# An attention and GLU block on one core: subtractions and stores of the down weights one key tile later, the guard's transpose one key tile sooner

## The chip, the cores and the metric

The kernel runs on one core of a Trainium2 chip. The metric is the device time of one execution in microseconds (us). A core has five engines: TensorE (PE, matrix products), VectorE (DVE), ScalarE (ACT), GpSimd (POOL) and SyncE (SP). Each runs its instructions in the order in which the program gives them, and they wait for one another through semaphores. SP issues nearly all transfers here; POOL issues some.

## What is computed

One block of a transformer in float32: layer norm, attention with 32 heads that share one key head and one value head, a residual sum, layer norm, a gated product without a nonlinearity, and a second residual sum. S = 2048 tokens, D = 576, head size 18, F = 4608.

```
x = A_x
h = x + attention(layernorm(x), wq, wk, wv, wo)   # softmax of q k / sqrt(18), keys and values shared by the 32 heads
n = layernorm(h)
out = h + ((n @ w_gate) * (n @ w_up)) @ w_down
```

## The kernel before

Queries are taken in four blocks of 512 tokens, heads in eight groups of four, keys in 16 tiles of 128. A **pair** (`pair`, line 674) is two heads of one group on one key tile: two score products of 56 rows each (line 694), then one exponential on ScalarE over 128 x 1024 numbers (line 695). Two pairs finish a key tile of a group, and `flush` (line 702) gives the value products of a finished key tile to PE (line 699), one key tile behind the scores. This stage, attention over the first query block, is where the change lies.

Beside the pairs, in the same stage, the loop in `run` (from line 1600) gives out three kinds of other work, and it is the program's own order on each engine that fixes when each is tried; no scheduler reorders it. One turn of the loop is a **step**: a pair, some query work, a pair, then waiting small jobs (`run_aux`, line 750), `flush`, and one `next(work)`, which is one step of the down weights.

- **Query work** (`queries`, line 473). The queries of all blocks are products of the normed tokens with the query weights, in tiles of 126 rows; each tile takes 14 rounds of two products (line 498, into the banks `psq` and `psr`, for the two halves of the rows). A round counts 1, the end of a tile 4, and a step hands out 2.3 (`RATE`, line 1659). At the end of a tile VectorE empties the banks: line 505 copies `psr`, line 506 adds `psq` to it, lines 507, 508 and 515 make the parts that are stored. The two banks come from one ring of two, so the next tile's first product into `psq` waits for line 505 and its first into `psr` for line 506. SP stores the tile (lines 510 and 511).
- **Bounds** (`bounds`, line 522). From each block's queries an upper bound of the scores is made, and its largest value is collected in `mx`. `flag` (line 562) reduces `mx` on DVE (line 566), transposes the result on PE (line 569, `psx`), and compares it (lines 571 and 573). Every engine reads that flag at the `guard` (lines 575 to 580), which branches around a repair that is not taken here. `flag` is a generator: `next(flag)` gives out the first reduction, `drain(flag)` the transpose and the rest.
- **Down weights** (`down_weights`, line 1491). In 18 blocks `p`, each of 128 x 4 x 288 numbers, the weights of the last product are loaded (`load`, by POOL, line 1515), combined (`sums`, POOL, line 1521), rounded to the format of the products (`high`, POOL's cast, line 1529), the rounding error is taken (`low(p, i)`, a subtraction on DVE, line 1535, in two spans `i`), and both parts go back to memory (`store`, two transfers by SP, line 1541), for the later stages to read. Block `p` is placed by `begin(p)`: step 6p up to block 10, then 5 apart. From there `load` stands 3 steps before (5 after block 10), `sums` at 0 and 1, `high` at 2, `low` at 4 and 5, `store` at 6. The room of a block is one of two up to block 9, of three after that, so the load of block p waits until store(p - 2), later store(p - 3), has landed.

After the loop, `run` gives out `next(flag)`, then two more steps, drains what is left of the down weights (nothing, the loop has 106 steps), gives out `drain(flag)`, goes on to the end of the seventh group, one pair of pairs more, and the guard.

Of the kernel before, what the change touches and what calls it, by code (L numbers as in the profile page):

```python
# [57 lines left out]
class Block:  # L58
# [1432 lines left out]
    def down_weights(self):  # L1491

        pool, dve, sp = self.nc.gpsimd, self.dve, self.sp
        rooms = [(self.hp.tile([P, 8, HD], F32, tag="h", name="wd_src"), self.hp.tile([P, 8, HD], F32R, tag="h", name="wd_hi"))]
        at, where = {}, {}

        def begin(p):  # L1500
            return 6 * min(p, 10) + 5 * max(p - 10, 0)

        def room(p):
            n = p % 2 if p < 10 else (2, 0, 1)[(p - 10) % 3]
            if p in (1, 5, 10):
                home, tag = {1: (self.otp, "oT"), 5: (self.p0q, "XT0"), 10: (self.p0q, "XT1")}[p]
                if p > 1:
                    self.XT[p // 5 - 1] = None
                e = home.tile([P, 9 * TB], F32R, tag=tag, name=f"wd_room{p}").rearrange("p (k j d) -> p k j d", k=2, d=HD)
                rooms[n:] = [(f32(e[:, 0]), e[:, 1])]  # L1510
            return rooms[n]

        def load(p):
            where[p] = room(p)
            pool.dma_start(where[p][0][:, 0:4], self.wd[p])

        def sums(p, i):
            src, _ = where[p]
            if p < NC - 1:
                for i, x, y in ((4, 0, 1), (5, 3, 4), (6, 3, 0), (7, 2, 5))[i:i + 2]:  # L1520
                    pool.tensor_tensor(src[:, i], src[:, x], src[:, y], ALU.subtract)

        def spans(p):
            return [(1, 4), (4, 8)] if p < NC - 1 else [(0, 4)]

        def high(p):
            src, hi = where[p]
            for lo, to in spans(p):
                pool.tensor_copy(hi[:, lo:to], src[:, lo:to])

        def low(p, i):

            src, hi = where[p]
            for lo, to in spans(p)[i:i + 1]:
                dve.tensor_tensor(src[:, lo:to], src[:, lo:to], f32(hi[:, lo:to]), ALU.subtract)

        def store(p):
            src, hi = where.pop(p)
            lo, to = spans(p)[0][0], spans(p)[-1][1]
            for k, t in enumerate((f32(hi), src)):  # L1540
                sp.dma_start(self.wd_dram[p, :, 0:to - lo, k], t[:, lo:to])
            if p in (3, NC - 2):
                del rooms[1:]

        for p in range(NC):
            if p > 10:
                at.setdefault(begin(p) - 5, []).insert(0, lambda p=p: load(p))
            else:
                at.setdefault(max(begin(p) - 3, -1), []).append(lambda p=p: load(p))
            for d, f in ((6, lambda p=p: store(p)), (0, lambda p=p: sums(p, 0)), (1, lambda p=p: sums(p, 2)),  # L1550
                         (2, lambda p=p: high(p)), (4, lambda p=p: low(p, 0)), (5, lambda p=p: low(p, 1))):
                at.setdefault(max(begin(p) + d, -1), []).append(f)
        for k in range(-1, max(at) + 1):
            for f in at.pop(k, ()):
                f()
            yield

    def run(self):
# [17 lines left out]
        with ExitStack() as st:  # L1576
            pool = lambda name, bufs, **k: st.enter_context(tc.tile_pool(name=name, bufs=bufs, **k))
            cp, self.lp, self.hp = pool("const", 1), pool("ln", 2), pool("resid", 2)
            self.qp, self.pp, self.op, self.otp = pool("q", 2), pool("P", P_BUFS), pool("o", 1), pool("oT", 1)
            self.ps = pool("ps", 1, space=PSUM)  # L1580
            self.C = cp.tile([P, C_W], F32, name="C")
            self.ident = self.C[:, C_ID:C_ID + P]
            self.kT = cp.tile([P, S], F32R, name="kT")
            self.V = cp.tile([P, NT, 32], F32, name="V")
            self.mx = cp.tile([H, 8], F32, name="mx")
            st.enter_context(tc.manual_schedule())
            with tc.tile_pool(name="p0q", bufs=1) as self.p0q:
                self.wq_in, self.wq = self.wq, {}
                self.XT = [self.p0q.tile([P, 9, TB], F32R, tag=f"XT{b}", name=f"XT{b}") for b in range(NB)]
                self.G = self.p0q.tile([P, 64], F32R, name="G")  # L1590
                with tc.tile_pool(name="qb", bufs=2) as self.qb:
                    first = self.keys_values()
                    work = self.down_weights()
                    next(work)

                    def rest():
                        yield from first
                        for b in range(1, NB):
                            yield from self.queries(b)
                    self.cast = self.dve.tensor_copy  # L1600
                    others, live, due = rest(), True, 0.0
                    while live:
                        self.pair()
                        due += RATE
                        while due > 0 and live:
                            z = next(others, None)
                            live = z is not None
                            due -= z or 0
                        self.pair()
                        self.run_aux(1)  # L1610
                        self.flush(len(self.pend) - 1)
                        next(work, None)
            assert self.n_mx <= 8
            flag = self.flag()
            next(flag)
            self.wp, self.hh, self.p2 = pool("w", 2), pool("hid", 4), pool("P2", P2_BUFS)
            n = self.n_pair + 4
            self.steps(lambda: self.n_pair < n, work)
            drain(work)
            drain(flag)  # L1620
            self.steps(lambda: self.n_pair % (2 * NT))
            assert self.n_pair == 2 * NT * (NG - 1)
            self.pair()
            self.pair()
            self.flush(len(self.pend) - 1)
            self.guard()
            wo_parts, n = self.load_wo_0(), self.n_pair
            self.load_x(0)
            self.wo_from = n + 12
            self.steps(lambda: self.n_pair < n + 8)  # L1630
            wo_parts()
            del wo_parts
            self.steps(lambda: self.more(0))
            self.load_w(0)
            self.load_wd(WD_BUFS - NQ)
            self.load_x(1)
            self.fill(2.0, 1)
            while 0 not in self.normed:
                self.run_aux(1)
                self.fill(1.0, 1)  # L1640
            while self.n_pair % 8 != 6:
                self.pair()
                if self.n_pair % 8 in (0, 2, 4):
                    self.flush(len(self.pend) - 1)
            self.normal(0)
            self.split_w(0)
            self.load_w(1)
            self.cast = self.act.copy
            drain(self.spread(0))
            self.flush(len(self.pend))  # L1650
            self.pair()
            del self.oT
            self.room()
            self.load_wd(WD_BUFS - 2)
            for b in range(NB - 1):
                self.ffn(b)
# [55 lines left out]
def f32(ap):  # L1712
    return ap.bitcast(F32)
# [20 lines left out]
def drain(gen):  # L1734
    for _ in gen:
        pass
# [85 lines left out]
```

## Time and profile before

| | |
|---|---|
| median of three runs | 2248.4 us (2247.45 to 2248.42) |
| the profiled execution | 2249.98 us, of which the span is 2248.1 us |
| PE busy | 2224.7 us, 99% of the span |
| ACT, DVE, POOL busy | 1436.3 us (64%), 1374.9 us (61%), 899.2 us (40%) |
| mean granted clock of PE | 0.998 |
| the chain that ended last, by engine | PE 85%, DVE 1%, all others about 0% |

The page counts as busy the time in which an engine executes; an instruction that waits for a semaphore is idle time, and the views name who ended it. PE at 99% says that the kernel is bounded by matrix products nearly throughout, so what can be gained is in PE's few gaps and in the stretches in which its clock is granted at less than full speed. Views in order of time merge equal instructions that follow one another into one line with a count.

### The profile page before, as it was taken

How to read it: one execution, taken by the hardware profiler on the slowest of the kernel's cores; microseconds unless marked ns; L12 is line 12 of the kernel's file. 1: busy time of each engine (PE TensorE's matmuls, PEld its weight loads, DVE VectorE, ACT ScalarE, POOL GpSimd, SP SyncE). 2: the span in 40 equal slices, each digit the busy share in tenths (PEclk: the TensorE clock that was granted, in tenths of full speed). 3: DMA queues.
4: the chain of work that ended last, by engine and by line, in shares of the span. 5: the costliest groups of instructions: out<-in, count | busy, mean ns of one | idle time of the engine just before them, and what ended most of it. 6: DMA issues, size and time to landing. Idle time of an engine off the chain costs nothing.

```text
span 2248.1 us, 45954 instructions
## 1 busy us (share of the span) xinstructions
PE 2224.7 (99%) x17958; PEld 1634.8 (73%) x17958; DVE 1374.9 (61%) x2209; ACT 1436.3 (64%) x1950; POOL 899.2 (40%) x976
## 2 busy tenths in 40 slices
PE   7999999999999999999999999999999999999999
PEld 5333335777777777777777777777777888999999
DVE  8555645555655566455555566546455677888776
ACT  7889877666666666666665667565666534555553
POOL 4445401444444444244444435433332455322222
PEclk9999999999999999999999999999999999999999
DMA  5879843545555554655455555564343445677775
GB/s 176 268 230 297 292 169 88 179 153 166 164 173 165 174 181 142 188 167 172 148 177 172 164 162 173 164 207 148 109 121 105 135 161 199 222 236 241 234 248 174
DMA packets 200625, 407.01 MB, mean 181 GB/s; under 512 B 22573, under 2 KB 54445, under 8 KB 200405
## 3 DMA queue, kind: packets, MB, share of 16 engines
q1 hardware_dynamic: 197813, 393.42, 54.6%
q0 software_dynamic: 2592, 10.62, 1.5%
q8 instruction: 143, 2.34, 0.4%
q14 instruction: 77, 0.63, 0.1%
HBM read 317.27 MB, written 74.55 MB: 174 GB/s over the span
## 4 chain that ended last, share of the span: by engine, by line
PE 85%; DVE 1%; ACT 0%; issue 0%; DMA 0%; POOL 0%; SPq 0%; ACTq 0%; DVEq 0%
PE pg L1106 19%; PE acc L699 16%; PE y L1046 13%; PE s L694 9%; PE gs L1332 8%; PE pu L1106 6%; PE yq L1298 4%; PE gu L1106 4%; PE yo L874 3%; PE gs L1339 2%; PE y L1013 1%; PE tx L936 0%; ACT P L695 0%; DVE room L97 0%; PE ye L1458 0%
## 5 line engine op out<-in xcount | busy, mean ns | idle before, releaser
L695 ACT ACTIVATE P<-s 128x1024 f32<-128x1024 f32 x1024 | 1010.1, 1028 | 218.5 <-PE s L694 134.7
L1106 PE MATMUL pg<-X,ws 64*128 64x512 f32 x2511 | 679.6, 389 | 0.5 <-DVE os L725 0.2
L1106 PE MATMUL pu<-X,ws 64*128 64x512 f32 x2511 | 679.8, 389 | 0.0
L1106 PEld LDWEIGHTS pg<-X,ws 64*128 64x128 f32 x2511 | 465.0, 185 | 65.9 <-issue 2.3
L699 PE MATMUL acc<-P,V 128*32 128x512 f32 x4096 | 481.3, 599 | 0.1
L1106 PEld LDWEIGHTS pu<-X,ws 64*128 64x128 f32 x2511 | 464.5, 185 | 16.7
L694 PE MATMUL s<-q,kT 56*128 56x512 f32 x2048 | 425.4, 415 | 5.8 <-ACT P L695 3.6
L1056 POOL TENSOR_TENSOR h<-h,tmp 128x288 f32<-128x288 f32 x320 | 259.1, 841 | 321.8 <-ACT tmp L1055 320.6
L1055 ACT COPY tmp<-y 128x288 f32<-128x288 f32 x320 | 127.9, 400 | 338.5 <-PE y L1046 308.7
L694 PEld LDWEIGHTS s<-q,kT 56*128 56x128 f32 x2048 | 197.8, 184 | 173.8 <-ACT P L695 124.9
L1046 PEld LDWEIGHTS y<-wdo,room 128*128 128x128 f32 x2142 | 289.4, 188 | 40.9 <-issue 38.2
L1046 PE MATMUL y<-wdo,room 128*128 128x288 f32 x2142 | 302.7, 300 | 0.1
L699 PEld LDWEIGHTS acc<-P,V 128*32 128x32 f32 x4096 | 114.4, 109 | 253.9 <-issue 250.8
L1052 DVE TENSOR_TENSOR h<-h,y 128x288 f32<-128x288 f32 x394 | 169.5, 453 | 181.8 <-PE y L1046 178.1
L971 DVE TENSOR_TENSOR ws<-wr,ws 128x1152 fp32r<-128x1152 f32 x108 | 188.7, 1747 | 105.0 <-POOL ws L968 103.6
L1144 DVE TENSOR_TENSOR hf<-pu,hf 128x512 f32<-128x512 f32 x93 | 63.7, 684 | 221.0 <-ACT hf L1140 221.0
L968 POOL CAST ws<-wr 128x1152 fp32r<-128x1152 f32 x108 | 130.8, 1211 | 146.8 <-DMA wr<-in_wgu_dram 119.6
L96 POOL CAST room<-hf 128x256 fp32r<-128x256 f32 (+1 forms) x92 | 58.5, 636 | 314.6 <-DVE hf L1144 314.6
L1281 POOL TENSOR_TENSOR wsum<-wsum,wsum 128x512 f32<-128x512 f32 x72 | 145.2, 2017 | 48.0 <-DMA wsum<-in_wgs_dram 36.0
L97 DVE TENSOR_TENSOR room<-hf,room 128x256 fp32r<-128x256 f32 (+1 forms) x108 | 96.1, 890 | 3.3 <-ACT room L96 1.8
L1106 PE MATMUL gu<-X,ws 64*128 64x512 f32 x810 | 94.5, 389 | 0.0
L1106 PEld LDWEIGHTS gu<-X,ws 64*128 64x128 f32 x810 | 76.5, 184 | 15.7 <-issue 1.3
(267 smaller groups left out, 2762.1 us busy)
## 6 DMA issues: line engine op xcount, KB each, us to landing
wdo<-wd_dram SPq DMA_DIRECT2D x492, 288.0 KB
wr<-in_wgu_dram SPq DMA_DIRECT2D x108, 576.0 KB
wsum<-in_wgs_dram SPq DMA_DIRECT2D x108, 256.0 KB
wd_dram<-wd_room SPq DMA_DIRECT2D x20, 1008.0 KB
wsum_dram<-wsum SPq DMA_DIRECT2D x72, 256.0 KB
raw<-wsum_dram SPq DMA_DIRECT2D x72, 256.0 KB
q<-q_dram SPq DMA_DIRECT2D x64, 216.0 KB
raw<-in_wgs_dram SPq DMA_DIRECT2D x54, 256.0 KB
```

The costliest lines, as they stand in the source:

```text
L694: self.pe.matmul(s_[:, i], self.kT[o:o + 56, t * P:(t + 1) * P], q[o:o + 56, pr], start=True, stop=True)
L695: self.act.activation(p_, s_, AF.Exp, scale=SCALE)
L699: self.pe.matmul(acc[32 * j:32 * j + 32, :], self.V[:, t, :], Ps[j // 2][:, j % 2, :], start=first, stop=last, skip_group_check=True)
L968: self.nc.gpsimd.tensor_copy(w[:, 0], self.wr[n])
L971: self.dve.tensor_tensor(w[:, 1], self.wr.pop(n), f32(w[:, 0]), ALU.subtract)
L1046: pe.matmul(y[:, :HD], m[:, t * P:(t + 1) * P], k, start=(first and j == 0), stop=(j == 2), skip_group_check=True)
L1052: dve.tensor_tensor(hs, hs, y[:, :HD], ALU.add)
L1055: act.copy(z, y[:, :HD])
L1056: pool.tensor_tensor(hs, hs, z, ALU.add)
L1106: pe.matmul(ps, w[o:o + 64, wk, c], X[o:o + 64, xk, c], start=(j == 0), stop=(j == 26))
L1281: pool.tensor_tensor(to, x, y, op)
L1332: pe.matmul(bank[:, g * HT:(g + 1) * HT], W[:, wk, c, g], X[:, 2 * xk + c], start=(first and g == c == wk == xk == 0), stop=(c == 1 and wk ...
```

## The change

Two constants in the placing of `store` and `low` grow by one, and one in the number of pairs before `drain(flag)` shrinks by two. `store(p)` goes from step begin(p) + 6 to + 7, the two subtractions from + 4 and + 5 to + 5 and + 6. Loads, sums and casts stay. `drain(flag)` comes after one step in place of two; the pairs themselves are unchanged in number.

```diff
--- before.py
+++ after.py
@@ -1547,8 +1547,8 @@
                 at.setdefault(begin(p) - 5, []).insert(0, lambda p=p: load(p))
             else:
                 at.setdefault(max(begin(p) - 3, -1), []).append(lambda p=p: load(p))
-            for d, f in ((6, lambda p=p: store(p)), (0, lambda p=p: sums(p, 0)), (1, lambda p=p: sums(p, 2)),
-                         (2, lambda p=p: high(p)), (4, lambda p=p: low(p, 0)), (5, lambda p=p: low(p, 1))):
+            for d, f in ((7, lambda p=p: store(p)), (0, lambda p=p: sums(p, 0)), (1, lambda p=p: sums(p, 2)),
+                         (2, lambda p=p: high(p)), (5, lambda p=p: low(p, 0)), (6, lambda p=p: low(p, 1))):
                 at.setdefault(max(begin(p) + d, -1), []).append(f)
         for k in range(-1, max(at) + 1):
             for f in at.pop(k, ()):
@@ -1614,7 +1614,7 @@
             flag = self.flag()
             next(flag)
             self.wp, self.hh, self.p2 = pool("w", 2), pool("hid", 4), pool("P2", P2_BUFS)
-            n = self.n_pair + 4
+            n = self.n_pair + 2
             self.steps(lambda: self.n_pair < n, work)
             drain(work)
             drain(flag)
```

## Rows read from the trace of the kernel before

**Rows 1.** TensorE's waits from 54 to 300 us: who waited for whom, us, times, longest us.

```profile
PE s L694 <- ACT P L695: 1.8, 7, 0.4
PE s L694 <- DVEq L580: 1.6, 1, 1.6
PE psq L498 <- DVE qs L505: 0.9, 1, 0.9
PE psr L498 <- DVE qs L506: 0.2, 1, 0.2
```

**Rows 2.** Busy us by engine in stretches, then PE clock, DMA share, GB/s.

```profile
136.18:139.60 3.42, 3.42 (x17) 1.29 (x16) 3.42 (x4) 1.41 (x2) 1.77 (x2) 0.50 0.74 251
...
300.02:303.44 3.42, 3.42 (x16) 0.70 (x12) 2.93 (x4) 2.20 (x3) 2.42 (x4) 0.50 1.03 398
```

**Rows 3.** TensorE in order of time around 134 us: start, us, operation [idle before <-releaser].

```profile
131.98 0.40 PE L498 MATMUL psq<-XT,wq 64*126 64x512 f32 x1
...
134.96 0.49 PE L498 MATMUL psq<-XT,wq 64*126 64x512 f32 x1 [0.92 <-DVE qs L505]
135.69 0.50 PE L498 MATMUL psr<-XT,wq 64*126 64x512 f32 x1 [0.23 <-DVE qs L506]
...
140.01 1.07 PE L699 MATMUL acc<-P,V 128*32 128x512 f32 x8
```

**Rows 4.** TensorE in order of time, another tile boundary, from 168 us.

```profile
168.31 0.39 PE L498 MATMUL psq<-XT,wq 64*126 64x512 f32 x1
...
171.00 1.07 PE L699 MATMUL acc<-P,V 128*32 128x512 f32 x8
...
173.12 1.06 PE L699 MATMUL acc<-P,V 128*32 128x512 f32 x8
```

**Rows 5.** VectorE in order of time, 96 to 150 us.

```profile
105.44 2.31 DVE L1535 TENSOR_TENSOR wd_room<-wd_room 128x864 f32<-128x864 f32 x2
115.32 0.69 DVE L505 COPY qs<-psr 126x512 f32<-126x512 f32 x1 [7.57 <-PE psr L498]
...
132.34 1.97 DVE L1535 TENSOR_TENSOR wd_room<-wd_room 128x864 f32<-128x864 f32 x1 [7.66 <-POOL wd_room L1529]
134.23 0.68 DVE L505 COPY qs<-psr 126x512 f32<-126x512 f32 x1
...
137.34 1.35 DVE L1535 TENSOR_TENSOR wd_room<-wd_room 128x1152 f32<-128x1152 f32 x1
```

**Rows 6.** VectorE in order of time, 150 to 200 us.

```profile
165.46 1.32 DVE L1535 TENSOR_TENSOR wd_room<-wd_room 128x1152 f32<-128x1152 f32 x1
168.75 0.69 DVE L505 COPY qs<-psr 126x512 f32<-126x512 f32 x1 [1.97 <-PE psr L498]
```

**Rows 7.** SyncE's queue in order of time, 50 to 110 us.

```profile
74.66 0.57 SPq L1541 DMA_DIRECT2D wd_dram<-wd_src  x1
75.67 3.25 SPq L1541 DMA_DIRECT2D wd_dram<-wd_room  x2
86.95 0.31 SPq L510 DMA_DIRECT2D q_dram<-qs  x1
```

**Rows 8.** GpSimd in order of time, 50 to 110 us.

```profile
82.19 0.57 POOL L1515 DMA_DIRECT2D wd_src<-in_wd_dram  x1 [6.55 <-DMA wd_dram<-wd_src]
...
94.96 0.57 POOL L1515 DMA_DIRECT2D wd_room<-in_wd_dram  x1
```

**Rows 9.** All engines in order of time at the flag and the guard.

```profile
290.54 1.06 PE L699 MATMUL acc<-P,V 128*32 128x512 f32 x8
290.56 0.15 DVE L566 TENSOR_REDUCE mx<-mx 32x1 f32<-32x7 f32 x1
...
293.88 0.18 PE L569 MATMUL psx<-C,mx 32*1 32x32 f32 x1
...
299.64 0.91 PE L694 MATMUL s<-q,kT 56*128 56x512 f32 x4 [1.57 <-DVEq L580]
```

**Rows 10.** The tile `flag`: reads of it, ns min/median/max, first and last start us.

```profile
L579 DVEq TENSOR_LOAD <-flag x1: 542/542/542, 298.1 to 298.1; - x1
```

## The prediction

> **What bounds the kernel now.** I read the page first and then, for the stretch that the diff touches, what ended TensorE's idle time. The change lies inside the first attention, whose loop runs from about 54 us to the guard at about 300 us of a span of 2248.1 us. In these 246 us TensorE (PE) waited for others 1.8 + 1.6 + 0.9 + 0.2 = 4.5 us [rows 1]. So this stretch is PE's own work, and an edit that moves only VectorE (DVE), GpSimd (POOL) and SyncE (SP) work can win no more than these 4.5 us and what follows from them. The reader should see three kinds: 1.8 us in 7 short waits for ScalarE, which are the pace of the softmax; 1.6 us in one wait at the guard; 0.9 + 0.2 us in one place, where PE waits for DVE to empty the two banks of a query tile. In the table by stretch, two stretches of 3.4 us show a granted clock of 0.50, that is 1.2 GHz in place of 2.4: one begins at 136.18 us, the other at 300.02 us [rows 2]. Each comes right behind one of these two waits: the queries' at 134.04 to 135.69 us, the guard's just before 299.64 us [rows 3, 9].
>
> **What the query wait costs now.** The same run of PE work, from the last products of a query tile to the third group of value products behind it, takes 140.01 - 131.98 = 8.03 us here [rows 3] and 173.12 - 168.31 = 4.81 us at another tile boundary [rows 4]. The difference is 3.2 us: 0.92 + 0.23 us of waiting, up to 3.42 / 2 = 1.7 us from the half clock, and the rest because the tile's two halves, issued as a pair, ran one after the other (134.96 and 135.69 us [rows 3]). PE is full on both sides, so I count all 3.2 us as path.
>
> Why DVE was late stands in its order. The last product ended at 131.98 + 0.40 = 132.38 us, but the copy that frees the first bank (line 505) began at 134.23 us, 1.85 us late [rows 3, 5]. Ahead of it stood a subtraction of block 5, low(5, 0). That one had kept DVE idle for 7.66 us, until POOL's cast of the same block came, and then ran 1.97 us [rows 5]. The other subtraction of that block, low(5, 1), came at 137.34 us, behind the tile's operations [rows 5].
>
> **The subtractions a step later.** Block p is due at begin(p) = 6p up to block 10, then 5 apart. low(5, 0) goes from step 34 to 35 and low(5, 1) from 35 to 36. Within a step the loop issues query work before down-weight work; low(5, 1) of step 35 stands behind this tile in the trace, so the tile belongs to step 35, and low(5, 0) now falls behind it too. DVE is then free at 132.4 us, the copy starts on time, and the 3.2 us go. low(5, 0) starts at about 132.4 + (137.34 - 134.23) = 135.5 us, its cast long done, and the pair ends some 2.3 us later (as the pair at 105.44 us [rows 5]), at 137.8 us, no later than before (137.34 + 1.3). Nothing downstream of block 5 is later for that.
>
> The other 34 subtractions: counted through the loop (2.3 units of query work a step, 17 units a tile, 28 of them left when it begins), the tiles' copies stand in steps 5, 13, 20, 27, 35, 42, 50, 57, 64, 72, 79, 86, 94 and 101. Only low(0, 0), low(5, 0), low(6, 1) and low(14, 1) pass behind a tile; none passes ahead of one. What moves closer to a tile is dangerous only if it ends late. Nearest is block 7: low(7, 0) goes from 46 to 47, behind the normalisation of that step, so that both subtractions begin where low(7, 1) began, at 165.46 us [rows 6]. With 2.31 us for a pair that DVE does alone [rows 5] they end at 167.8 us; the copy of that tile is due at 168.75 us [rows 6], so 0.95 us is left. With 1.97 us for the first, as beside a POOL cast [rows 5], they end at about 168.75 us, just in time. I take the first: POOL waits for a transfer there. (The Trainium skill, "SBUF — State Buffer", section "Who interferes with whom", says that a DVE instruction with two inputs in SBUF contends with a GpSimd one that reads SBUF, and that issue order decides who blocks; the 1.97 against about 1.0 us agree. By it the later place, with the casts done, makes the subtractions shorter, and the sum stays as it is.)
>
> **The stores a step later.** A step is about 2.1 us (171.00 to 173.12 [rows 4]). Each of the 36 store transfers goes behind what SP is given in the next step. The largest slip is store(1), from step 12 to 13, where a query tile's store stands first in the queue: from 75.67 us to behind the transfers at 86.95 us, so to about 88 us [rows 7]. POOL's load of block 3 reuses that room and waits for it. store(0)'s second transfer began at 74.66 us and released POOL at 82.19 us, 7.5 us [rows 7, 8]; with that, store(1) is landed at about 96 to 97 us and the load goes out 1 to 2 us later than at 94.96 us [rows 8]. low(3, 0) at 105.44 us was not waiting for POOL [rows 5], and behind that pair DVE is idle for 7.57 us before the next tile at 115.32 us [rows 5], which covers the slip. Later stores wait for DVE or for query stores in the queue now and slip a step or less. Cost: 0 on the path; without that cover each us is paid as under the ring below. Query and mask stores and ob copies, which were behind a store, go a little earlier; no PE wait names them [rows 1].
>
> **The flag's transpose two pairs sooner.** Nothing is added or removed. The products it now follows end at 290.54 + 1.06 = 291.60 us; the maximum it reads is done at 290.56 + 0.15 = 290.71 us [rows 9], so it has 0.9 us to spare; if DVE were later than that, PE with the score products behind it would wait the rest. It frees SP and POOL at the guard some 2 us sooner, and the loads of the output weights with them; no PE wait in [rows 1] is theirs. It doesn't shorten the guard: PE starts again at 299.64 us when DVE has passed its branch [rows 9], and DVE reads the flag only at 298.1 us [rows 10], 4 us after the transpose at 293.88 us [rows 9], because the last accumulator's transpose stands ahead of it. I count 0; between -0.2 and +0.2 us, its own length of 0.18 us [rows 9], as it leaves a full place or lands in one.
>
> **Sum.** -3.2 + 0 + 0 + 0 = -3.2 us. The profiled execution took 2249.98 us for a span of 2248.1 us, so it would be 2246.8; against the median of the three runs, 2248.4 us, I forecast 2245.2 us. My own range for this case is 2244.4 to 2246.2.
>
> **Rivals.**
> The half clock behind the guard goes too: if the stretch at 300.02 us ran at the full clock, up to another 3.42 / 2 = 1.7 us is won, 2243.5 us. Against it: the guard's wait stays as it is.
>
> The half clock behind the queries is not in the median run: then only 3.2 - 1.7 = 1.5 us is won, 2246.7 us. For it: three runs within 1 us can't tell. (The Trainium skill, "TensorE: Matmul & The Clock Gate", section "What's actually happening", says that where the clock changes isn't tied to the kernel's start and varies from run to run; by that rule this rival or the last can hold. The trace shows one execution and neither agrees nor disagrees.)
>
> The stall only moves: block 7's pair ends 1 us late and PE stalls at the tile of 168.75 us instead, or the change reaches nothing on PE: 2248.4 us.
>
> Slower, through the ring of rooms. Up to block 9, block p's load waits for store(p - 2). Two such waits are in [rows 8]: 6.55 us at 82.19, and 94.96 us with none. If every store slips its whole step of 2.1 us and no slack takes it up, block 7, three turns on, is 6.4 us late: 166.8 + 6.4 = 173.2 us for the end of low(7, 1), and the copy due at 168.75 us is 4.4 us late. At 134.23 us a copy 1.85 us late cost 3.2 us, 1.35 us more than its lateness, so this costs 5.8 us and the net is +2.6 us, 2251.0 us. It decides from the point where low(7, 1) ends after 168.75 us. Against it: the slack found at block 3.
>
> **How the numbers follow.** What a measurement of this kernel can tell from no change is about 0.2%, 4.5 us. Forecast 0.60; guard's clock too 0.12; only 1.5 us 0.08; stall moves or nothing 0.12; ring 0.08. Faster by over 0.2% is below 2243.9 us: nearly all of the second case, 0.12. Slower by over 0.2% is above 2252.9 us: a ring that also reaches the tile after next, 0.04. Within: 0.84. The range takes in the forecast's own bounds, the guard's clock and the cases around no change: 2243.2 to 2249.0 us; outside stay the ring and little more.
>
> **What would show it.** Right: no PE wait for the queries' copies at about 134 us, low(5, 0) behind that tile on DVE, the run of PE work 4.8 us long, a granted clock of 1.00 there, the guard's wait near 1.6 us. Wrong: a new PE wait for line 505 or 506 at a tile boundary; DVE waits for POOL's casts of blocks 6 to 9 that grew; a wait of PE for the maximum at the flag's transpose; or all this as said and a time that didn't move.

## The result, and the profile after

| | before | after |
|---|---|---|
| median | 2247.2 us (15 runs, 2244.81 to 2251.52) | 2252.2 us (15 runs, 2250.14 to 2256.23) |
| the profiled execution | 2249.98 us, span 2248.1 | 2256.23 us, span 2253.9 |
| mean granted clock of PE | 0.998 | 0.996 |

The ratio is 1.0024, 95% interval [1.0016, 1.0032]: the change costs 4.9 us where I had forecast a gain of 3.2. Both profiled executions lie above their medians, before by 2.7 us and after by 4.1 us, so a size read from one of them is not yet the size of the median.

TensorE's waits from 54 to 310 us in the profile after (who waited for whom, us, times, longest us), to be held against [rows 1]:

```profile
PE psq L498 <- DVE qs L505: 3.4, 1, 3.4
PE s L694 <- ACT P L695: 3.1, 8, 1.4
PE s L694 <- DVEq L580: 1.6, 1, 1.6
```

Three things are to be seen. The wait for line 506 is gone, and the one for line 505 is 3.4 us long in place of 0.9, at another tile. The waits for ScalarE have grown, and one of them is 1.4 us long where none was above 0.4. The guard's 1.6 us stand. In order of time on TensorE (start, us, operation, idle before and its releaser), the old place and the new one:

```profile
131.88 0.40 PE L498 MATMUL psq<-XT,wq 64*126 64x512 f32 x1
...
136.69 1.07 PE L699 MATMUL acc<-P,V 128*32 128x512 f32 x8
...
146.99 0.39 PE L498 MATMUL psq<-XT,wq 64*126 64x512 f32 x1
...
154.35 0.79 PE L498 MATMUL psq<-XT,wq 64*126 64x512 f32 x1 [3.42 <-DVE qs L505]
...
156.65 1.94 PE L699 MATMUL acc<-P,V 128*32 128x512 f32 x8
...
160.27 1.06 PE L699 MATMUL acc<-P,V 128*32 128x512 f32 x8
```

At the old place the run from the last query products to the third group of value products now takes 136.69 - 131.88 = 4.81 us, to the hundredth what another boundary took [rows 4], and no longer 8.03 [rows 3]. The forecast gain is there. It is given back 14 us later: at the next tile, whose last products start at 146.99 us, PE stops for 3.42 us, and then matrix products take 0.79 and 1.94 us that take 0.39 and 1.06 elsewhere. The table by stretch (start:end, length, busy us of PE, of the weight loads, DVE, ACT, POOL with their counts, granted clock, DMA share, GB/s) says why:

```profile
134.00:140.00 6.00, 6.00 (x46) 2.19 (x46) 4.76 (x7) 5.63 (x7) 0.57 (x1) 1.00 1.03 350
153.09:159.92 6.83, 5.57 (x20) 2.46 (x22) 5.49 (x7) 1.50 (x2) 3.58 (x4) 0.50 0.64 214
303.28:310.10 6.82, 5.67 (x24) 1.43 (x24) 6.09 (x10) 3.75 (x4) 3.76 (x5) 0.50 0.91 333
```

The half clock of 136.18 us [rows 2] is gone (1.00), but one of 6.83 us begins within the new wait, and the one at the guard is 6.82 us long, not 3.42. From 146.99 to the fourth group of value products, at 160.27 us, the boundary takes 13.28 us. Where it isn't disturbed (the experiment with low(6, 0) below) the same run takes 6.70 us: a loss of 6.6 us against the 3.2 won. The longer half clock at the guard adds (6.82 - 3.42) / 2 = 1.7 us: -3.2 + 6.6 + 1.7 = 5.1 of the 5.8 us by which the two spans differ. The guard's part can't be put down to the change, since the clock falls there in some profiles and not in others whatever the edit (last section).

VectorE says why PE waited (to be held against [rows 5]):

```profile
132.32 0.69 DVE L505 COPY qs<-psr 126x512 f32<-126x512 f32 x1 [4.52 <-PE psr L498]
...
135.44 2.32 DVE L1535 TENSOR_TENSOR wd_room<-wd_room 128x864 f32<-128x864 f32 x2
...
151.73 1.97 DVE L1535 TENSOR_TENSOR wd_src<-wd_src,wd_hi 128x864 f32<-128x864 f32 x1 [12.91 <-POOL wd_hi L1529]
153.62 0.68 DVE L505 COPY qs<-psr 126x512 f32<-126x512 f32 x1
```

At 132 us all is as forecast: the copy comes first, the pair of block 5 behind it, at 135.44 us (I had said 135.5). But low(6, 0) stands ahead of the next tile's copy, as it did before the change, and now it keeps DVE idle for 12.91 us until POOL's cast of block 6 comes. The tile was finished at 146.99 + 0.39 = 147.38 us; its copy starts at 153.62 us, 6.2 us late.

The cast is late because load 6 is, and load 6 because store(4) is. First the kernel before, on GpSimd and in SyncE's queue, neither of which stands ahead of the prediction for this stretch:

```profile
133.87 0.57 POOL L1515 DMA_DIRECT2D wd_src<-in_wd_dram  x1 [0.47 <-issue]
...
142.23 1.99 POOL L1529 CAST wd_hi<-wd_src 128x864 fp32r<-128x864 f32 x2
```

```profile
119.72 0.53 SPq L1541 DMA_DIRECT2D wd_dram<-wd_hi  x1
123.10 0.52 SPq L1541 DMA_DIRECT2D wd_dram<-wd_src  x1
...
128.48 5.55 SPq L796 DMA_DIRECT2D ob<-ob  x4
```

Then the kernel after, the same two engines (to be held against [rows 7, 8] too):

```profile
99.04 0.57 POOL L1515 DMA_DIRECT2D wd_room<-in_wd_dram  x1 [6.95 <-DMA wd_dram<-wd_room]
...
110.68 0.57 POOL L1515 DMA_DIRECT2D wd_src<-in_wd_dram  x1 [2.05 <-DMA wd_dram<-wd_src]
...
122.02 1.99 POOL L1529 CAST wd_hi<-wd_src 128x864 fp32r<-128x864 f32 x2
...
139.03 0.57 POOL L1515 DMA_DIRECT2D wd_src<-in_wd_dram  x1 [5.59 <-DVE oT L97]
...
150.79 2.00 POOL L1529 CAST wd_hi<-wd_src 128x864 fp32r<-128x864 f32 x2
```

```profile
88.15 2.47 SPq L1541 DMA_DIRECT2D wd_dram<-wd_room  x2
...
127.83 3.09 SPq L796 DMA_DIRECT2D ob<-ob  x4
131.02 0.58 SPq L1541 DMA_DIRECT2D wd_dram<-wd_hi  x1
131.70 0.61 SPq L1541 DMA_DIRECT2D wd_dram<-wd_src  x1
...
136.65 3.29 SPq L1541 DMA_DIRECT2D wd_dram<-wd_room  x2
```

Read from the bottom: store(4) was out at 119.72 and 123.10 us; now it stands behind four `ob` copies that SyncE doesn't issue before 127.83 us, and goes out at 131.02 and 131.70 us, 11.3 and 8.6 us later for a move of one step. Load 6, which reuses its room, goes out at 139.03 in place of 133.87 us (5.2 later), and from there to the cast it is 11.8 us in place of 8.4. Together the cast is 8.6 us late. (The view names `oT L97` as the releaser of load 6. That VectorE operation runs far from the room. In all six profiles with a cast 6 past 148 us load 6 goes out 7.3 us behind the issue of store(4)'s second transfer, here 139.03 - 131.70, and in three of them the view names that store; the experiments below show that it is store(4).)

The `ob` copies wait for the normalisation of a finished group, whose last operation is line 787 (VectorE of the kernel after):

```profile
122.95 3.24 DVE L1535 TENSOR_TENSOR wd_src<-wd_src,wd_hi 128x864 f32<-128x864 f32 x2 [1.67 <-POOL wd_hi L1529]
...
127.09 0.71 DVE L787 STREAM_TRANSPOSE ob<-os 128x512 f32<-128x512 f32 x1
```

Line 787 ran at 123.97 us before. Now it stands behind low(4, 0) and low(4, 1), which waited 1.67 us for their own cast, since load 4 too was late (110.68 in place of 105.88 us). So the lag of the earlier stores comes in here a second time, by way of VectorE.

At the guard, all engines in order of time (to be held against [rows 9]):

```profile
294.79 0.18 PE L569 MATMUL psx<-C,mx 32*1 32x32 f32 x1
...
299.38 3.77 ACT L695 ACTIVATE P<-s 128x1024 f32<-128x1024 f32 x4 [1.89 <-SPq L580]
```

The flag's transpose waits for nothing. ScalarE waits 1.89 us here before its first exponential behind the flag, and PE the 1.4 us that the waits show.

### The profile page after: what moved, and what is told of

It is laid out like the page before. It is cut to its first block, busy times and chain, and to the rows that moved or that the text cites. A ratio compares the mean times of both kernels' runs of the same rounds, so it can differ in the third digit from the quotient of the medians.

```text
span 2253.9 us, 45955 instructions
## 1 busy us (share of the span) xinstructions
PE 2226.8 (99%) x17958; PEld 1631.3 (72%) x17958; DVE 1373.4 (61%) x2209; ACT 1435.1 (64%) x1950; POOL 897.0 (40%) x976
## 4 chain that ended last, share of the span: by engine, by line
PE 84%; DMA 1%; DVE 1%; ACT 0%; issue 0%; POOL 0%; SPq 0%; ACTq 0%; DVEq 0%
PE pg L1106 20%; PE acc L699 15%; PE y L1046 13%; PE s L694 9%; PE gs L1332 8%; PE pu L1106 5%; PE yq L1298 4%; PE gu L1106 4%; PE yo L874 3%; PE gs L1339 2%; PE y L1013 1%; DMA q<-q_dram 0%; PE tx L936 0%; ACT P L695 0%; DMA wo_r<-in_wo_dram 0%
## 5 line engine op out<-in xcount | busy, mean ns | idle before, releaser
L97 DVE TENSOR_TENSOR room<-hf,room 128x256 fp32r<-128x256 f32 (+1 forms) x108 | 95.1, 880 | 3.3 <-ACT room L96 1.8
```

## The experiments

My theory after the two traces was that the stores' slip does the harm, through the ring of rooms; the rivals were that the subtractions' own move does it, or the flag's. From the second group of kernels on, with that settled, the letters in the quoted expectations stand for what each of them spells out. Each kernel is timed beside the kernel before; "wait at the tile of block 6" is PE's wait at about 150 us. The last two columns are read from one execution each, the profiled one; the whole timeline of one execution can lie up to 2 us sooner or later than that of another.

| kernel | median us | ratio to before, 95% | load 6 out, cast 6, us | wait at the tile of block 6, us |
|---|---|---|---|---|
| before, its second profile | 2247.8 | 1.0002 [0.9993, 1.0011] | 133.37, 141.68 | none |
| the change | 2252.2 | 1.0024 [1.0016, 1.0032] | 139.03, 150.79 | 3.42 |
| flag only | 2246.9 | 0.9996 [0.9987, 1.0005] | 131.52, 140.25 | none |
| subtractions only | 2246.7 | 0.9996 [0.9987, 1.0005] | 129.75, 139.03 | none |
| stores only | 2253.6 | 1.0024 [1.0014, 1.0035] | 138.33, 148.88 | 2.29 + 0.23 |
| low(5, 0) only | 2246.6 | 0.9993 [0.9984, 1.0002] | 132.58, 140.48 | none |
| change, low(6, 0) behind the tile | 2247.1 | 0.9998 [0.9989, 1.0008] | 138.30, 150.12 | none |
| change, store(4) back | 2245.5 | 0.9991 [0.9982, 1.0000] | 134.36, 142.47 | none |
| change, store(1) back | 2250.1 | 1.0007 [0.9998, 1.0016] | 137.34, 148.71 | 1.30 + 0.24 |
| change, stores 11 to 17 back | 2252.0 | 1.0025 [1.0016, 1.0034] | 136.74, 148.47 | 2.78 |
| change, store(5) later still | 2252.1 | 1.0024 [1.0015, 1.0033] | 136.82, 148.63 | 2.85 + 0.23 |
| before, store(4) alone later | 2248.6 | 1.0009 [1.0000, 1.0018] | 135.18, 143.37 | none |
| change without its stores | 2244.2 | 0.9989 [0.9980, 0.9998] | 128.55, 139.44 | none |

The last two columns sort the kernels: where cast 6 starts past 148 us and low(6, 0) stands ahead of the tile, the wait is there and the median is above 2250 us; everywhere else it is below 2249.

**The three parts, one at a time.**

```
flag only:          n = self.n_pair + 4   ->   n = self.n_pair + 2
subtractions only:  low at +4, +5         ->   +5, +6     (store stays at +6, given out behind low)
stores only:        store at +6           ->   +7
```

> Only the flag's transpose goes one step sooner; subtractions and stores stay where they were. The trace of the changed kernel has, at the guard, a TensorE wait of 1.42 us for an exponential that it did not have before, and a longer stretch at the half clock behind it, about 2.4 us together. Theory A, the ring of rooms (the stores' slip in SyncE's queue makes everything behind late, the first exponential in the second pool among it): the flag has no part in it, 2247.2 us like the kernel before (within 0.7 us), no such wait. Theory C, the flag's new place makes SyncE or ScalarE wait there: about 2249.6 us, and the wait of 1.4 us is there.

> Only the 35 subtractions go one step later; each store stays at step begin(p) + 6, in the same place of SyncE's queue as before, behind its subtraction. Theory A (the stores' slip did the harm): the wait for the copy at 134 us goes and nothing comes in its place, no TensorE wait at the tile of 147.4 us, GpSimd's load of block 6 goes out at 134 to 135 us, 2247.2 - 3.2 = 2244.0 us. Theory B (the later subtractions hold the rooms longer and VectorE waits for later casts): load of block 6 at 137 us or later, a wait at 147 to 154 us, 2250 us or more.

> Only the stores go one step later; the subtractions stay. Theory A: the load of block 3 goes out at about 99 us and that of block 6 at about 139 us as in the changed kernel; the wait for the copy at 134 us stays as before, so TensorE comes to the tile of block 6 some 3.3 us later and waits there about 3.4 - 3.3 us or a little, up to 1.5 us; with the wait of 1.4 us at the guard 2249 to 2252 us. Theory B: stores alone change nothing, 2247.2 us.

The stores alone have the whole loss, 1.0024, and the wait at the tile of block 6 (2.29 us), although the subtractions stand where they stood. The flag alone and the subtractions alone each end at 0.9996, which can't be told from nothing. Two sizes were missed: the subtractions alone came to 2246.7 where the theory that held said 2244.0 us, and the stores alone waited longer than the 1.5 us expected and took 2253.6 us, 1.6 above the expected range. So the rivals fall, and the long wait for ScalarE at the guard, which is in neither the stores-only profile nor any other but that of the change, is not needed for the loss.

**The one subtraction that I had counted the gain on.**

```
low(p, 0) at +4 -> +4 + (p == 5)
```

> One subtraction alone, the first of block 5, goes one step later, behind the copies of the query tile that ends at 132.4 us; all else as before. Every theory: the wait of 0.92 + 0.23 us at 134 us and the half clock behind it go, 2247.2 - 3.2 = 2244.0 us; if the half clock is not there in most executions, 2245.7 us. If the time stays at 2247.2 us, the gain that the trace of the changed kernel shows at 134 us (the value products 3.3 us earlier) is given back later by itself, and the account by offsets falls.

0.9993 [0.9984, 1.0002]: at most 3.6 us, and at its middle 1.6 us, nearer to the smaller of the two gains expected. The wait at 134 us is not in its profile. Why the gain comes out smaller than 3.2 us, the profile of the kernel with the flag alone suggests, where low(5, 0) stands in its old place too (VectorE in order of time):

```profile
126.76 1.97 DVE L1535 TENSOR_TENSOR wd_room<-wd_room 128x864 f32<-128x864 f32 x1 [1.56 <-POOL wd_room L1529]
...
132.39 0.69 DVE L505 COPY qs<-psr 126x512 f32<-126x512 f32 x1 [3.66 <-PE psr L498]
```

There low(5, 0) started 5.6 us sooner than in [rows 5] and was over by 128.7 us, and VectorE waited for PE, not PE for it. The flag-only kernel gives out the same program as the kernel before until its flag, at about 290 us, so the wait that I priced is one that an execution may have or not.

**The kernel before once more**, to see whether it has.

```
(no edit)
```

> The kernel before itself, as a second profile of it. Theory A (the query wait at 134 us and the half clock behind it come in some executions only, by when the transfer of block 5 lands): cast 5 on GpSimd ends either at about 128 us, and TensorE then waits for no copy at 134 us, or at about 133 us with the wait of 0.9 us. Rival: it is in every execution, and cast 5 again ends past 133 us with a wait of about 0.9 us. Time 2247 us, ratio 1.000 within 0.001 either way.

TensorE in order of time, and the table of the stretch behind it:

```profile
134.45 0.49 PE L498 MATMUL psq<-XT,wq 64*126 64x512 f32 x1 [1.31 <-DVE qs L505]
135.17 0.79 PE L498 MATMUL psr<-XT,wq 64*126 64x512 f32 x1 [0.23 <-DVE qs L506]
```

```profile
135.06:141.89 6.83, 6.72 (x27) 2.05 (x27) 5.16 (x7) 3.07 (x3) 4.59 (x5) 0.50 0.86 304
```

The wait is there again, 1.31 + 0.23 us, and the half clock there is twice as long as in [rows 2]. So far this fits the rival as well, that every execution of this kernel has it; but this execution, too, lies 2.7 us above its run's median (2250.47 against 2247.82 us), and the rest of the evidence comes from the other kernels. Of the five profiles with low(5, 0) in its old place (these two, the flag alone, the stores alone, store(4) alone) four have a wait, of 0.7 to 1.5 us, and two of those no half clock. With the flag alone the cast was early because load 5 landed sooner. The trace's list of transfers for that load (tiles, KB, us to landing), in the kernel before and then with the flag alone:

```profile
wd_room<-in_wd_dram POOLq DMA_DIRECT2D x1, 576.0 KB, 8.5
```

```profile
wd_room<-in_wd_dram POOLq DMA_DIRECT2D x1, 576.0 KB, 4.5
```

Before, load 5 goes out at 119.64 us, 0.9 us behind the store of the queries at 118.72 us; with the flag alone it went out at 117.80 us, 1.1 us ahead of that store at 118.89 us. In the eight profiles in which load 5 goes out near that store it is the same: 8.2 to 8.8 us to land in the four where load 5 goes out 0.9 us behind the queries' store (both of the kernel before, low(5, 0) only, store(4) alone), 4.5 to 4.7 us in the four where it goes out 0.6 to 1.2 us ahead (flag only, subtractions only, store(1) back, without stores). In the other six load 5 goes out 5.5 to 7.0 us behind it and lands in 3.9 to 6.3 us. That the order of the two issues is the cause is not shown: no run changed it alone. Full DMA engines are not the whole of it either: their share while load 5 was under way was 0.94 before and 0.68 with the flag alone, but only 0.71 with store(4) alone, where the load took 8.2 us. With the stores alone late, load 5 landed fast (4.2 us) and cast 5 was late for the lag of the ring.

**Where the harm is paid.** The change with low(6, 0) a step later still, behind the tile of block 6, and nothing else:

```
low(p, 0) at +5 -> +5 + (p == 6)
```

> The changed kernel with one more edit: low(6, 0) stands at step + 6, so that it is given out behind the query tile of block 6 and can't stand ahead of that tile's copies. All stores stay a step later, so load 6 still waits for a late store(4). Theory B (the harm is paid at one place: low(6, 0), whose cast is late, stands ahead of the copy of line 505): TensorE's wait of 3.4 us at 151 us and the half clock behind it go, and about the forecast time comes out, 2246 to 2248 us. Theory C (the late ring pays in several places, and the tile of block 6 is only the first): the wait appears at the next tile or at the guard, and the time stays at 2250 to 2252 us.

2247.1 us, 5.1 us below the change, as the first theory said. The ring is as late as before (cast 6 at 150.12 us), but nobody on the path waits for it any more (VectorE, then TensorE):

```profile
147.34 0.69 DVE L505 COPY qs<-psr 126x512 f32<-126x512 f32 x1 [7.63 <-PE psr L498]
...
151.95 3.26 DVE L1535 TENSOR_TENSOR wd_src<-wd_src,wd_hi 128x864 f32<-128x864 f32 x2
```

```profile
146.91 0.39 PE L498 MATMUL psq<-XT,wq 64*126 64x512 f32 x1
...
153.61 1.07 PE L699 MATMUL acc<-P,V 128*32 128x512 f32 x8
```

153.61 - 146.91 = 6.70 us is the undisturbed run used above. One subtraction in one place carries the loss.

**Which stores make it late.** The change with one store, or the last seven, back at their old step:

```
store(p) at +7 -> 7 - (p == 4)
store(p) at +7 -> 7 - (p == 1)
store(p) at +7 -> 7 - (p >= 11)
```

> The changed kernel with store(4) alone back at step + 6, given out last in its step, ahead of the four ob copies of the next step on SyncE. Theory B (one issue, store(4) held behind four ob copies, makes load 6 late): GpSimd's load 6 goes out at about 134 to 136 us in place of 139, cast 6 ends by about 145, no wait at the tile of block 6, 2246 to 2248 us. Theory C (the lag has built up since store(1), and load 6 would be late anyway, or its landing is what is slow): load 6 at 137 us or later, a wait of 1 us or more remains at about 151 us, 2249 to 2252 us.

> The changed kernel with store(1) alone back at step + 6, where it stands ahead of the query store on SyncE. Load 3 should go out at about 95 us again in place of 99. Theory A (the lag of block 3 is carried on to block 6): load 4 and load 6 go out earlier by 2 us or more, the wait at 151 us shrinks to under 1.5 us, 2246.5 to 2249 us. Theory B (each late store pays by itself; the lag of block 3 is taken up before block 6): load 6 at about 139 us as in the changed kernel, the wait of about 3.4 us stays, 2251 to 2253 us.

> The changed kernel with the stores of blocks 11 to 17 back at step + 6 and those of blocks 0 to 10 still a step later. Theory B (the price is paid at block 6 alone): the time stays at 2251 to 2253 us, and the profile keeps the wait at about 151 us and loses ScalarE's wait of 1.9 us for the first exponential in the new pool. Theory D (the late stores at the end, which hold the guard's surroundings, carry a third or more of the harm): 2249 to 2250.5 us. If the end were all of it: 2247 us.

With store(4) back (SyncE, then GpSimd) its second transfer is ahead of the copies again and load 6 five microseconds sooner:

```profile
125.64 0.52 SPq L1541 DMA_DIRECT2D wd_dram<-wd_src  x1
...
130.21 4.32 SPq L796 DMA_DIRECT2D ob<-ob  x4
```

```profile
134.36 0.57 POOL L1515 DMA_DIRECT2D wd_src<-in_wd_dram  x1 [0.63 <-DVE qs L508]
...
142.47 2.00 POOL L1529 CAST wd_hi<-wd_src 128x864 fp32r<-128x864 f32 x2
```

The wait goes and 6.7 us with it, all of the loss and more (half a us more than was expected). With store(1) back, load 3 goes out at 94.00 us again, and part of that is left at block 6, where the view names the store itself as the releaser:

```profile
94.00 0.57 POOL L1515 DMA_DIRECT2D wd_room<-in_wd_dram  x1
...
137.34 0.57 POOL L1515 DMA_DIRECT2D wd_src<-in_wd_dram  x1 [8.59 <-DMA wd_dram<-wd_src]
...
148.71 1.99 POOL L1529 CAST wd_hi<-wd_src 128x864 fp32r<-128x864 f32 x2
```

Load 6 is 1.7 us sooner than in the change, in an execution whose tile comes at the same time (its last products at 147.02 us, 146.99 in the change). Line 787 runs at 125.41 in place of 127.09 us and the `ob` copies go out at 126.15 in place of 127.83 us, so it is by the normalisation that the lag reaches store(4). (The 136.74 and 136.82 us of two other rows are sooner only because those executions run 1.6 to 1.7 us ahead. Measured from the last products of the tile at about 114 us, load 6 comes 22.5 us behind here, 24.3 in the change, and 23.6 in the three others that have store(1) and store(4) late and low(5, 0) behind its tile.) The wait is 1.30 + 0.24 us in place of 3.42, and the medians differ by 2.1 us, though the two intervals touch at 1.0016. Neither expectation fits whole: the lag of block 3 is carried on, but by under half. The last seven stores carry nothing: with them back the loss is 1.0025. 

**Is store(4) enough by itself?**

```
kernel before: store(p) at +6 -> 6 + (p == 4)
```

> The kernel before with store(4) alone a step later, behind the four ob copies on SyncE; all else stays. Theory B (this one issue is enough): load 6 at 136 to 138 us, to cast 6 some 11.5 us, low(6, 0) ahead of the copy of the tile that ends at about 147 us, a wait of 1 us or more there; 2249.5 to 2251.5 us. Theory C (it takes the lag of block 3 as well): under 0.5 us of wait, 2247 to 2248.5 us.

```profile
135.18 0.57 POOL L1515 DMA_DIRECT2D wd_src<-in_wd_dram  x1 [3.00 <-DVE qs L507]
...
143.37 1.99 POOL L1529 CAST wd_hi<-wd_src 128x864 fp32r<-128x864 f32 x2
```

```profile
144.30 3.24 DVE L1535 TENSOR_TENSOR wd_src<-wd_src,wd_hi 128x864 f32<-128x864 f32 x2 [5.76 <-POOL wd_hi L1529]
147.98 0.69 DVE L505 COPY qs<-psr 126x512 f32<-126x512 f32 x1 [0.45 <-PE psr L498]
```

Not in this execution: load 6 is out at 135.18 us, and low(6, 0) and its pair end 0.45 us before the copy's data is there. But it took 2246.36 us, among the fastest of a run that reaches 2252.33 us; with so little to spare, slower ones may have the wait. The ratio is 1.0009 [1.0000, 1.0018], and by it store(4) alone can't be told from the change with store(1) back. The whole loss, 1.0024, takes store(4) behind the copies and the lag that the other stores bring.

**Why load 6 also lands later.**

```
store(p) at +7 -> 7 + (p == 5)
```

> The changed kernel with store(5) another step later, at step + 8, so that its two transfers no longer lie beside load 6. Theory B1 (load 6 lands 8.5 us after its issue, in place of 3.7 us, because store(5) shares the DMA engines with it): load to cast of block 6 falls from 11.8 to about 8.5 us, cast 6 ends at about 149 in place of 152.8 us, the wait at 151 us falls below 0.5 us; 2247 to 2249 us, unless load 7, which waits for store(5), makes a wait at the next tile. Theory B2 (it is store(4) itself, still moving, that load 6 shares the engines with): load to cast stays at 11 to 12 us, the wait of about 3 us stays, 2251 to 2254 us.

The edit moved nothing: store(5) went out right behind the query tile's store, as in the change.

```profile
134.99 2.36 SPq L1541 DMA_DIRECT2D wd_dram<-wd_room  x2
```

So this run says nothing on its question, and repeats the change within its spread. What the other profiles show: where load 6 goes out ahead of store(5), it lands in 3.7 to 5.5 us (eight profiles, 3.7 in the kernel before), and where it goes out 1.5 to 2.4 us behind it, in 7.3 to 8.5 us (the six with a cast 6 past 148 us). Behind the two transfers of store(5), of 1008 KB each, those of store(4) are also not long out, so which of the two slows the load stays open. The DMA engines were full while it was under way: a share of 1.02 at 338 GB/s from 139.03 to 147.53 us in the change, 0.57 at 185 GB/s from 133.87 to 137.57 us in the kernel before.

**The change without its stores**, as the version that these point to:

```
low at +5, +6; n = self.n_pair + 2; store at +6, given out behind low
```

> The change without its stores: both subtractions a step later and the flag's transpose a step sooner, the stores where the kernel before has them (behind the subtraction of the same step). Theory A (the stores alone do the harm, the other parts are worth under 1 us together): 2245.5 to 2247.5 us, no wait for a query copy at 134 or 151 us, GpSimd's load 6 at 129 to 135 us. If the query wait of 3.2 us read from the profile of before were in most of its executions: 2244 us or less.

2244.2 us, ratio 0.9989 [0.9980, 0.9998]: 2.6 us faster than the kernel before, 8 us faster than the change, and the fastest of all; that lies between the two times expected. Its profile has no wait for a query copy and a granted clock of 1.00 from 54 to 310 us, and its load 5 is out at 114.96 us, 1.2 us ahead of the queries' store.

## Why the prediction was wrong

**The query wait and its cause: right; its size in the median: too large.** The chain (cast 5 late, low(5, 0) ahead of the copy, PE waiting) and the place of every operation at 132 to 136 us came as told. The 3.2 us are those of one execution that lay 2.7 us above its median. Without the stores the change gains 2.6 us [0.4, 4.5]; low(5, 0) alone 1.6 us, with an interval that reaches zero. The rival "only 1.5 us", to which I gave 0.08, lies nearest to the middle of the second, though both intervals take in 3.2 as well. (The Trainium skill, "TensorE: Matmul & The Clock Gate", section "What's actually happening", on which it leant, says that where the clock changes varies from run to run. The two profiles of the kernel before agree: 3.42 us of half clock at this wait in one, 6.83 in the other.)

**The stores at no cost: this step failed.** I took store(1) for the largest slip, found load 3 "1 to 2 us later" covered, and wrote of the rest "slip a step or less". store(1) did go out at "about 88 us" (88.15), but landed only at 99.04 us, not at 96 to 97, and load 3 went out then, 4.1 us later than in [rows 8]. At block 3 the cover still held: no wait followed there. And store(4) slipped 11.3 and 8.6 us, four to five steps, since the step it was moved past holds the four `ob` copies, which stand in SyncE's queue until the normalisation behind a group's end is done. With the lag from block 3, a fifth to a third of it (the 1.1 to 1.7 us above), that made 5.2 us at load 6, another 3.4 us to the cast, and 6.6 us on PE in the profiled execution; taking store(4) back won 6.7 us in the median, taking low(6, 0) out of the way 5.1 us. I had measured the slip in steps of the order; a queue measures it by what the instructions in between wait for. I looked that up for one of eighteen stores.

**The other subtractions: I looked at the wrong ones.** I went through those that pass behind a tile, and of the others only through block 7, as the one that ends closest to a copy. low(6, 0) stays ahead of its tile; before, its pair left VectorE 4.34 us of idle time ahead of the copy at 150.74 us (VectorE of the kernel before):

```profile
143.16 3.24 DVE L1535 TENSOR_TENSOR wd_src<-wd_src,wd_hi 128x864 f32<-128x864 f32 x2 [2.31 <-POOL wd_hi L1529]
150.74 0.69 DVE L505 COPY qs<-psr 126x512 f32<-126x512 f32 x1 [4.34 <-PE psr L498]
```

That was the cover of every store up to store(4), and it was never weighed against a lag. A cast 8.6 us late was twice that. And the gain itself brought the tile forward: its copy was due at 147.38 us, 3.4 us sooner than the 150.74 us of before, so only about 1 us of the cover was left. With low(6, 0) behind the tile the median is 0.9998 of the one before, and the loss is gone.

**The rival of the ring: right in kind, wrong in place and chance.** It had the loads waiting for stores, a late subtraction ahead of a copy, and 2251.0 us against the measured 2252.2. It put the stall at block 7, with a lag that grows evenly; it came at block 6, by one large slip on top of a small lag. I gave it 0.08 on the strength of the slack at block 3, which is slack of another block.

**The flag: right.** No wait for the maximum, no change at the guard, 0.9996 by itself. The chance of 0.04 for "slower" stood on the same slack as the ring's.

## What to carry to other kernels

A transfer that is moved by one place in a queue is moved behind everything that the instructions of that place wait for: read, for each of them and not only for the first, when the queue could issue what now stands ahead. Where buffers go round in a ring, follow the lag of a late release to the first instruction on an in-order engine that stands ahead of something the critical engine needs; the idle time just before that one, less what the change brings the critical engine forward, is the whole cover. And read a gain off two executions, since a wait of a microsecond for a transfer can be in one and not in the other.

## What the hardware showed that I had not expected

Loads 5 and 6, of 576 KB each, landed in 3.7 to 5.5 us where they went out 0.5 to 4.7 us ahead of SyncE's next store, in 7.3 to 8.8 us where they went out 0.9 to 2.4 us behind one, and in 3.9 to 6.3 us where they went out 5.5 us or more behind. So a shift of some 2 us between issues on two engines went with 4 us in what waits for the load. Other loads of the same traces took anything from 3.5 to 12.0 us, so this holds for these two alone. (The Trainium skill, "DMA: Bandwidth & Descriptors", section "Issuing engines are not separate DMA queues", says that transfers issued by different engines end on the same 16 DMA engines and interleave; the DMA share of 1.02 while the change's load 6 took 8.5 us, against 0.57 while that of before took 3.7, agrees. Load 5 with store(4) alone, 8.2 us at a share of 0.71, is not explained by it.)

At the guard's wait of 1.6 us, the same in all fourteen profiles, the granted clock fell to 0.50 in seven and stayed at 1.00 in seven, and where it fell it was for 3.4 us in four and for 6.8 us in three. So the same wait costs its own length, or 1.7 or 3.4 us more. No edit here decided which.
